# Batch 0 of a fused attention and MLP kernel: one head pair per load on two queues, an order that keeps one port apart, and w_in issued behind q

## The chip, the cores and the metric

The kernel runs on one core of one Trainium2 chip. The metric is the device time of one execution in microseconds (us), as a median over several executions. The core has five engines that run side by side, each through its own queue in order: TensorE (PE in the profile, its weight loads PEld), VectorE (DVE), ScalarE (ACT), GpSimd (POOL) and SyncE (SP, here only DMA issues). DMAs are issued from SP's, ACT's and POOL's queues; those of POOL can change the type on the way (float32 to bf16).

## The reference

```
scale = 1 / sqrt(sqrt(64))                  # q, k, v: 8 batches x 8 heads x 576 x 64
phi(x) = exp(h - max(h)) / sqrt(128),  h = x @ omega.T - |x|^2 / 2
kv  = phi(k).T @ v;   z = sum(phi(k))
att = (phi(q) @ kv) / (phi(q) @ z + 1e-6)
x   = att, heads side by side               # 4608 x 512
h   = x @ w_in                              # 512 x 2048
out = (h * clip(h + 3, 0, 6) / 6) @ w_out   # 2048 x 512, float32 out
```

The row factor of phi(q) drops out of num / den, so q's maximum isn't computed. k's row factor is kept as one reciprocal per row of k, and is multiplied into v.

## The kernel before

One list of operations is written down for all eight batches (`_emit`), each with its engines, an estimated duration, a priority, what it reads and what it writes. `Prog.schedule` (L104) then goes through it with a model of the chip and fixes, before anything runs, on which engine each operation is and in which order each engine takes its own. What is fixed is the order alone: at run time an operation starts when its engine has come to it and the semaphores that it waits for are there. Matmuls on a tile of ones (`idle_work`, L463, "fills") are put on PE by the planner where it thinks PE would have nothing to do; they keep PE's clock up, and take their time even where the planner was wrong.

A batch is 576 rows of 8 heads: four pairs of heads (m = 0 to 3, `NP`), for each pair 512 rows of each head in the "mains" and 64 in the "left-overs" (`l`). For batch 0, names as used in this document (the digit after the first point is the batch, the one after that the pair):

- `load` (L491) issues the DMAs of k, q, v as float32; batch 0 has the list `FIRST` (L337): k's mains, k's left-overs, q's mains, v's left-overs, v's mains, q's left-overs. Each mains DMA is one head of two pairs (`HALVES`), 256 KB. The first four DMAs go alternately to SP and ACT, the rest to SP.
- `cast` (L573) makes bf16 of k and q (castk, castq), `turns` (L576) transposes on PE (Tk, Tq) and copies back from PSUM (Tevk, Tevq).
- K0.u (L639, two matmuls each, nine groups of four chunks) projects k; eK0.u (L645, ACT) is the exponential; mx0.u (L648, DVE) the maximum; cc.0.m (L746) and ccl (L675) are reciprocals.
- vc.0.m (L750) multiplies v by the reciprocals, 128x512; vcl (L679, two instructions) does that for the left-overs; vcc (L754) writes the reciprocals beside them.
- Q0 (L656, PE) and eQ0 (L660, ACT) do q's side.
- kv.0.m (L763, L765) needs vc.0.m, vcc.0.m and vcl; kvz.0.m (L417 or L418) copies it from PSUM; num.0.mA and B (L791) multiply with phi(q), A and B being the first and second half of the rows; rec and div (L803, L807, DVE) divide; X.0.mA and B (L429) transpose the result and Xev copies it to xT.
- mm1 (batch 0: `mm1_half`, L884, in halves 0A and 0B of the rows; later L859) and mm2 (L917) are the two matmuls of the MLP. A batch's MLP runs beside the attention of the next.

`w_in_piece` (L474) and `w_out_piece` (L481) issue the weights from POOL's queue, four pieces of 512 KB each (wi0 to wi3, wo0 to wo3). wi0 and wi1 wait for v's left-overs of batch 0, wi2 and wi3 for v's last mains (`W_GATE`, L339). Batch 1's k, q, v wait for wi1, wi2, wi3, and w_out waits for batch 1's k. From batch 1 on k and q are cast by POOL's DMAs; from batch 2 on the transposes are DMAs too.

The lists of engines that an operation may go to are `EV0` (L16) for batch 0 and `EV_V` and others (L344 to L350) after it: vc and vcl may go to POOL or DVE. The planner takes, of the operations that an engine could start next, the one of the best priority among those that could start within `URGENT` (0.8 us) of the earliest, and puts another in front if that ends at most `FIT` (0.05 us) after it could start (L198 to L202).

Of the kernel before, what the change touches and what calls it, by code (L numbers as in the profile page):

```python
# [5 lines left out]
BF16 = mybir.dt.bfloat16  # L6
# [5 lines left out]

URGENT = 0.8
FIT = 0.05
IDLE_UNTIL = 21.0
# [27 lines left out]
class Prog:  # L43
# [60 lines left out]
    def schedule(self):  # L104
# [9 lines left out]
        queues = {}  # L114
        clock = [0.0]

        def flow(until, keep):
# [55 lines left out]
        while len(order) < n:  # L173
            best = None
            for e, lst in engines.items():
                cand = []
                for o in lst:
                    s = slot_of(o) if o.alloc else (0.0, ())
                    if s is None:
                        continue  # L180
                    cand.append((max(free[e], ready(o), s[0]), o, s[1]))
                if not cand:
                    continue
                idle = [x for x in cand if x[1].name == "idle"]
                cand = [x for x in cand if x[1].name != "idle"]
                m = min([x[0] for x in cand] + [1e9])
                if idle and (not cand or idle[0][0] + (0.02 if idle[0][0] < 8.0 else idle[0][1].occ) <= m):
                    if idle[0][0] > IDLE_UNTIL:
                        if not cand:
                            continue  # L190
                    elif best is None or idle[0][0] < best[0]:
                        best = (idle[0][0], e, idle[0][1], idle[0][2])
                        continue
                    else:
                        continue
                if not cand:
                    continue
                c = min((x for x in cand if x[0] <= m + (URGENT if x[1].prio < -1.0 else 0.02)),  # L198
                        key=lambda x: (x[1].prio, x[1].seq))
                fits = [x for x in cand if x[0] + (x[1].occ[e] if isinstance(x[1].occ, dict) else x[1].occ) <= c[0] + FIT]  # L200
                if c[0] > m + 0.02 and fits:
                    c = min(fits, key=lambda x: (x[1].prio, x[1].seq))  # L202
                if best is None or c[0] < best[0]:
                    best = (c[0], e, c[1], c[2])
            if best is None and all(o.name == "idle" for l in engines.values() for o in l):
                break
            if best is None:
                raise RuntimeError("stuck: " + str([(e, [o.name for o in l][:5]) for e, l in engines.items()]))
            st, e, o, picks = best
            for x in o.engs:  # L210
                engines[x].remove(o)
            o.eng = e
            occ = o.occ[e] if isinstance(o.occ, dict) else o.occ
            for vx, i in zip(o.alloc, picks):
                old = vx.ring.held[i]
                if old is not None:
                    for d in old.users:
                        o.deps.setdefault(d, False)
                vx.slot = i
                vx.ring.held[i] = vx  # L220
            o.start = st
            if o.group is not None:
                free[e] = st + o.issue
                flow(free[e], True)
                queues.setdefault(e, []).append([o, occ, free[e] + (1.25 if e == "POOL" else 0.9)])
                flow(1e9, False)
            else:
                free[e] = st + occ
                o.end = free[e]
            for vx in o.virts:  # L230
                vx.left -= 1
                vx.free_at = max(vx.free_at, o.end + o.lat)
            order.append(o)
            for s in o.succ:
                s.ndep -= 1
                if s.ndep == 0:
                    add(s)
# [81 lines left out]
def _emit(nc, es, q, k, v, omega, w_in, w_out, out):  # L319
# [13 lines left out]
    TU = [(0, 2), (2, 6), (6, 10), (10, 14), (14, 18)]  # L333
    HALVES = [(0, 2), (2, 4)]
    SPLIT = 3
    LATE = 0.4
    FIRST = [("k", 1), ("k", 0), ("q", 1), ("v", 0), ("v", 1), ("q", 0)]  # L337
    REST = [("k", 1), ("k", 0), ("q", 1), ("q", 0), ("v", 0), ("v", 1)]
    W_GATE = [("vl", 0)]*2+[("v32", 1, 3)]*2  # L339
    alpha = float(D) ** -0.25  # L340
    PE_T, PE_X = 2, 2
    SPARE = 1
    IDLE = (16, 60)
    EV_T = ("DVE", "ACT")  # L344
# [25 lines left out]
    kp = [sbt("kp%d" % u, [128, NCH, M], BF16) for u in range(2)]  # L370
    mx = [sbt("mx%d" % u, [128, NCH], F32) for u in range(2)]
    cc = [sbt("cc%d" % u, [128, NCH], F32) for u in range(2)]
    vc = [sbt("vc%d" % u, [128, 520], BF16) for u in range(2)]
# [100 lines left out]
    def w_in_piece(i, gate):  # L474
        f0, f1 = WI[i]
        op("POOL", 0.72 * (f1 - f0), lambda E: E.dma_start(
            wi[:, :, 128 * f0:128 * f1], w_in[:, 128 * f0:128 * f1].rearrange("(c p) f -> p c f", p=128)),
           -8.6 + 0.05 * i, reads=gate, writes=[("wi", i)], group="dwi%d" % i, inc=16, lat=1.0, name="wi%d" % i,
           issue=0.85, packet=91.0)

    def w_out_piece(g, gate):  # L481
        op("POOL", 2.95, lambda E: E.dma_start(
            wo[:, 4 * g:4 * g + 4, :], w_out[512 * g:512 * g + 512, :].rearrange("(c p) e -> p c e", p=128)),
           -0.2 + 0.05 * g, reads=gate, writes=[("wo", g)], group="dwo%d" % g, inc=16, lat=1.0, name="wo%d" % g,
           issue=0.85, packet=91.0)
# [5 lines left out]
    def load(b, eng, gates):  # L491
        pb = b % 2
        halves = HALVES if b == 0 else [(0, NP)]
        turn_of = [0]

        def dma(part, dst, src, n, keys, gate, prio, run):
            cast = b > 0 and part[0] in "kq"
            e = "POOL" if cast else eng[turn_of[0]] if turn_of[0] < len(eng) else "SP"
            op(e, n * (0.74 if b == 0 else 0.8) * (1.0 if run == 1024 else 1.5) / 262144.0,
               lambda E: E.dma_start(dst, src), prio + 0.001 * turn_of[0], reads=gate + (free if cast else []), writes=keys,  # L500
# [15 lines left out]
        def mains(t, src, dst):  # L516
            for x, (m0, m1) in enumerate(halves):
                for hh in range(2):
                    first = 64 * hh if t != "q" else 0
                    d = dst[:].rearrange("p m (h r) d -> p m h (r d)", h=2) if t == "v" else mains_of(dst)  # L520
                    rows = src[b, 2 * m0 + hh:2 * m1 - 1 + hh:2, first:first + MAIN, :]
                    dma("%s%d%d" % (t, hh, x), d[:, m0:m1, hh, :], rows.rearrange("m (p r) d -> p m (r d)", r=4),
                        131072 * (m1 - m0), landing(t, hh, m0, m1), gates[t], base[t], 1024)

# [20 lines left out]
    def attention(b):  # L545
# [19 lines left out]

        def four(m0, m1, hh):
            return [2 + 4 * m + 2 * hh + s for m in range(m0, m1) for s in range(2)]

        def every(m0, m1, s):
# [20 lines left out]

        def dbls(t):
            return t[:, 2:, :].rearrange("p (m h s) t -> p m h (s t)", h=2, s=2)

        def alts(t, s, m0, m1):
# [8 lines left out]
        if b == 0:  # L603
            for m0, m1 in HALVES:
                for hh in range(2):
                    nm = "%d%d" % (m0 // 2, hh)
                    dbl = four(m0, m1, hh)
                    cast("k", nm, 512, mains_of(kb)[:, m0:m1, hh, :], mains_of(k32)[:, m0:m1, hh, :],
                         main_keys("k", range(m0, m1), [hh]), dbl, 0)
                    turns("k", nm, dbl, dbls(kT)[:, m0:m1, hh, :], kb, 0)  # L610
            for s in range(2):
# [22 lines left out]
        for u in range(NU):  # L634
            vK = Virt(ring)

            def e_K(E, u=u, vK=vK):
# [9 lines left out]
               pos(u) + 0.02, reads=[vK], writes=[("kp", pb, u)], name="eK%d.%d" % (b, u))  # L647
            op("DVE", dvet(512), lambda E, u=u: E.reduce_max(  # L648
                mx[pb][:, 4 * u:4 * u + 4], kp[pb][:, 4 * u:4 * u + 4, :], axis=AX.X),
               pos(u) + 0.03, reads=[("kp", pb, u)], writes=[("mx", pb, u)], name="mx%d.%d" % (b, u))  # L650

# [25 lines left out]
        for hh in range(2):  # L677
            p0 = 64 * hh
            op(EV_V if b else V0, {"POOL": 0.62, "DVE": dvet(260)}, lambda E, hh=hh, p0=p0: E.tensor_tensor(  # L679
                vcl[pb][p0:p0 + 64, :, 65 * hh:65 * hh + 65], vl[pb][p0:p0 + 64, :, :],  # L680
# [57 lines left out]
    def pair(b, m, t):  # L738
# [10 lines left out]
        vcm = vc[u2][:].rearrange("p (c e) -> p c e", e=65)  # L749
        op(EV_V if b else V0, {"POOL": 1.2, "DVE": dvet(512)}, lambda E: E.tensor_tensor(  # L750
            vcm[:, :, 0:D], v32[:, m, :, :], cbc, ALU.mult),
# [187 lines left out]
    for b in range(B):  # L939
        if b == 0:  # L940
            load(0, ("SP", "ACT", "SP", "ACT"), {t: [] for t in "kqv"})
            for i in range(len(WI)):
# [72 lines left out]
```

The softmax here doesn't subtract the row's maximum and nothing guards it: scores larger than these inputs give would overflow.

## Time and profile before

| | |
|---|---|
| median of 6 runs | 323.96 us (323.75 to 325.13) |
| the profiled execution | 324.21 us, of which the span of instructions is 322.4 us |
| granted clock of PE over the span | 1.00 |
| busy: PE, DVE, ACT, POOL | 317.2, 209.1, 189.1, 77.0 us |

The profile shows one execution. A group of instructions is shown by line of the kernel, engine, operation and tile; "xcount" is how many, "mean ns" the length of one. Matmuls overlap, so that their own lengths are longer than the distance from one to the next: a 128x256 matmul is shown with 273 ns, and 14 of them take 1.73 us. Windows are stretches of the span, in us from its start. In a timeline a line stands for instructions of one kind in a row: its start, how long they take together, and in brackets how long the engine stood idle before them and what it waited for.

### The profile page before, as it was taken

How to read it: one execution, taken by the hardware profiler on the slowest of the kernel's cores; microseconds unless marked ns; L12 is line 12 of the kernel's file. 1: busy time of each engine (PE TensorE's matmuls, PEld its weight loads, DVE VectorE, ACT ScalarE, POOL GpSimd, SP SyncE). 2: the span in 40 equal slices, each digit the busy share in tenths (PEclk: the TensorE clock that was granted, in tenths of full speed). 3: DMA queues.
4: the chain of work that ended last, by engine and by line, in shares of the span. 5: the costliest groups of instructions: out<-in, count | busy, mean ns of one | idle time of the engine just before them, and what ended most of it. 6: DMA issues, size and time to landing. Idle time of an engine off the chain costs nothing.

```text
span 322.4 us, 5873 instructions
## 1 busy us (share of the span) xinstructions
PE 317.2 (98%) x2236; PEld 174.8 (54%) x2236; DVE 209.1 (65%) x460; ACT 189.1 (59%) x385; POOL 77.0 (24%) x107
## 2 busy tenths in 40 slices
PE   8999999999999999999999999999999999999996
PEld 6788855455654544565555545555555444444443
DVE  4988995597787947995796468846866353433411
ACT  3997892596595616966775387647674354344400
POOL 2775171065041600730334022402020000000000
PEclk9999999999999999999999999999999999999999
DMA  7999989999950999898929972998012201000024
GB/s 246 265 204 212 235 130 233 230 166 193 217 129 36 123 201 256 94 189 126 238 24 173 200 219 33 184 199 232 16 50 66 74 23 45 33 35 33 33 67 98
DMA packets 91532, 44.79 MB, mean 139 GB/s; under 512 B 58096, under 2 KB 87024, under 8 KB 91504
## 3 DMA queue, kind: packets, MB, share of 16 engines
q1 hardware_dynamic: 64288, 31.31, 42.4%
q0 software_dynamic: 26512, 12.46, 31.2%
q10 hardware_dynamic: 704, 0.66, 0.6%
q8 instruction: 18, 0.29, 0.4%
q14 instruction: 10, 0.08, 0.1%
HBM read 36.73 MB, written 9.44 MB: 143 GB/s over the span
## 4 chain that ended last, share of the span: by engine, by line
PE 92%; DVE 2%; DMA 2%; SPq 2%; POOL 1%; issue 0%; ACT 0%; POOLq 0%
PE p L917 39%; PE p L859 34%; PE p L656 5%; PE p L884 4%; PE p L639 4%; PE p L791 3%; PE p L763 2%; DMA v<-in_v_dram 2%; SPq L500 2%; DVE mx L648 1%; PE p L429 1%; PE p L765 1%; DVE vc L750 0%; POOL vc L750 0%; DVE vcl L679 0%
## 5 line engine op out<-in xcount | busy, mean ns | idle before, releaser
L917 PE MATMUL p<-wo,gT 128*128 128x512 bf16 (+2 forms) x592 | 141.0, 374 | 0.3 <-DVE qT L418 0.3
L867 DVE SCALAR_TENSOR_TENSOR gT<-tsb,p 128x512 bf16<-128x512 bf16 x128 | 86.8, 685 | 56.7 <-ACT tsb L865 55.9
L865 ACT ACTIVATE tsb<-p 128x512 bf16<-128x512 f32 x128 | 76.3, 602 | 71.1 <-PE p L859 71.0
L859 PE MATMUL p<-xT,wi 128*128 128x512 bf16 x448 | 107.3, 379 | 0.0
L917 PEld LDWEIGHTS p<-wo,gT 128*128 128x128 bf16 x592 | 56.2, 98 | 57.5 <-DVE qT L418 0.5
L859 PEld LDWEIGHTS p<-xT,wi 128*128 128x128 bf16 x448 | 42.6, 98 | 45.4
L648 DVE TENSOR_REDUCE mx<-kp 128x4 f32<-128x512 bf16 x72 | 46.7, 673 | 9.7 <-ACT kp L645 9.4
L645 ACT ACTIVATE kp<-p 128x512 bf16<-128x512 f32 x72 | 40.0, 621 | 15.2 <-PE p L639 15.1
L660 ACT ACTIVATE qpT<-p 128x512 bf16<-128x512 f32 (+1 forms) x80 | 41.6, 576 | 5.2 <-PE p L656 5.0
L750 POOL TENSOR_TENSOR vc<-v,cc 128x512 bf16<-128x512 f32 x22 | 23.5, 1067 | 36.9 <-DVE cc L746 27.4
L807 DVE TENSOR_TENSOR xb<-p,rec 128x384 bf16<-128x384 f32 (+1 forms) x64 | 28.5, 477 | 0.0
L639 PE MATMUL p<-om,kT 128*128 128x256 bf16 x144 | 23.0, 273 | 0.0
L656 PE MATMUL p<-qT,om 128*128 128x512 bf16 (+1 forms) x80 | 22.8, 358 | 0.0
L418 DVE COPY osb<-p 128x512 f32<-128x512 f32 (+2 forms) x12 | 7.8, 647 | 22.7 <-PE p L917 22.7
L417 ACT COPY osb<-p 128x512 f32<-128x512 f32 x25 | 14.8, 591 | 11.3 <-PE p L917 11.3
L639 PEld LDWEIGHTS p<-om,kT 128*128 128x128 bf16 x144 | 13.8, 98 | 9.7
L500 POOL DMA_DIRECT2D k<-in_k_dram x12 | 9.1, 770 | 41.6 <-PE p L859 33.7
L791 PEld LDWEIGHTS p<-kvz,qpT 128*128 128x128 bf16 x312 | 13.5, 98 | 5.8 <-ACT qpT L660 0.2
L859 PE MATMUL p<-xS,wi 128*128 128x512 bf16 x64 | 16.4, 379 | 0.0
L884 PE MATMUL p<-xT,wi 128*128 128x256 bf16 x128 | 15.9, 273 | 0.0
L763 PEld LDWEIGHTS p<-vc,kp 128*128 128x128 bf16 x256 | 11.9, 98 | 6.6 <-POOL vcl L679 0.7
L791 PE MATMUL p<-kvz,qpT 128*128 128x65 bf16 x312 | 14.8, 194 | 0.0
(69 smaller groups left out, 216.6 us busy)
## 6 DMA issues: line engine op xcount, KB each, us to landing
out_dram<-osb SPq DMA_DIRECT2D x32, 256.0 KB, 2.7
v<-in_v_dram SPq DMA_DIRECT2D x14, 512.0 KB, 5.3
wi<-in_moe_w_in_dram POOLq DMA_DIRECT2D x4, 512.0 KB, 8.1
k<-in_k_dram POOLq DMA_DIRECT2D x8, 256.0 KB, 5.3
k<-in_q_dram POOLq DMA_DIRECT2D x8, 256.0 KB, 6.5
wo<-in_moe_w_out_dram POOLq DMA_DIRECT2D x4, 512.0 KB, 13.3
kb<-in_k_dram POOLq DMA_DIRECT2D x6, 256.0 KB, 5.7
qb<-in_q_dram POOLq DMA_DIRECT2D x6, 256.0 KB, 7.8
```

Of the source, the lines that this page charges most:

```text
L639: ins = E.matmul(ring.t[vK.slot][:, 256 * i:256 * i + 256], kT[:, 2 * u + i, :], om[:].rearrange("d t m -> d (t m)"), start=True, stop=True)
L645: op("ACT", actt(512), lambda E, u=u, vK=vK: E.activation(kp[pb][:, 4 * u:4 * u + 4, :].rearrange("p c m -> p (c m)"), ring.t[vK.slot], AF ...
L648: op("DVE", dvet(512), lambda E, u=u: E.reduce_max(mx[pb][:, 4 * u:4 * u + 4], kp[pb][:, 4 * u:4 * u + 4, :], axis=AX.X), pos(u) + 0.03, r ...
L656: op("PE", mmt(n), lambda E, vQ=vQ, lh=lh: E.matmul(ring.t[vQ.slot][:, 0:n], om[:, lh, :], src, start=True, stop=True), p + 0.045 * lh, re ...
L660: op("ACT", actt(n), lambda E, vQ=vQ, lh=lh: E.activation(dst(lh), ring.t[vQ.slot][:, 0:n].rearrange("m (j t) -> m j t", t=128), AF.Exp, s ...
L791: ins = E.matmul(d[:, hh, i - i0, :], qpT[pb][:, o:o + 128], kvz[m][:, 65 * hh:65 * hh + 65], start=True, stop=True)
L807: op("DVE", dvet(128 * n), lambda E: E.tensor_tensor(xv(i0, i1), psum()[:, :, :, 0:64], rbc, ALU.mult), t + 0.01, reads=[vn, ("rec", ru)], ...
L859: ins = E.matmul(ring.t[vh.slot], wi[:, c, 128 * f:128 * f + 128], xv[:, c, :], start=(c == 0), stop=(c == NJ - 1))
L865: op("ACT", actt(512), lambda E: E.activation(tsb[tu][:], ring.t[vh.slot], AF.Relu, bias=0.5, scale=1.0 / 6.0), t - 0.1, reads=[vh], write ...
L867: op("DVE", dvet(512), lambda E: E.scalar_tensor_tensor(gT[gu][:, f, :], tsb[tu][:], 1.0, ring.t[vh.slot], ALU.min, ALU.mult), t - 0.1, re ...
L884: ins = E.matmul(ring.t[vh.slot][:, 256 * g:256 * g + 256], wi[:, c, 128 * (f + g):128 * (f + g) + 128], xT[0][:, c, 256 * half:256 * half ...
L917: ins = E.matmul(ring.t[vo.slot][:, 0:c1 - c0], gT[gu][:, f, 128 * tc:128 * tc + 128], wo[:, f, c0:c1], start=(f == 0), stop=(f == NF - 1))
```

## The change

- Batch 0's loads: k's pairs 0 and 1 come one head of one pair per DMA (128 KB), pairs 2 and 3 both heads of one pair per DMA (256 KB); q's as before, one head of two pairs; v's both heads of one pair. The first eight DMAs alternate between SP and ACT (four on ACT: k's head 1 of pairs 0 and 1, k's pair 3, q's first), the rest is on SP. k's casts and transposes in batch 0 follow these pieces (`KPARTS`).
- All four pieces of w_in wait for q's last mains.
- The planner: a POOL operation is not started before DVE's last operation named vc, vcl, cast or fold has ended, and such a DVE operation not before POOL's last. PE's operations are counted twice as long between 4 and 6 us. `URGENT` goes to 0.5, `FIT` to 0.1, and some estimated durations change (vc on POOL 1.2 to 1.32, vcl 0.62 to 0.72, the weights' DMAs).
- A folded form of the maximum is written down for batches below `FOLD`; `FOLD` is 0, so there is none.

Because the planner decides, each engine's order changes from the start to the end of the kernel. What the builds of both kernels hold for batch 0:

| | before | after |
|---|---|---|
| fills on PE | 63 | 65 |
| fills ahead of the first Tk | 18 | 14 |
| vc.0 on POOL, on DVE | 1, 3 | 4, 0 |
| vcl.0 on POOL | 2 | 2 |
| POOL, from its second castq | castq0.0B, wi0, wi1, vcl x2, wi2, wi3, castq0.1B, vc.0.2, castq0.l | castq0.0B, wi0 to wi3, vc.0.0, vcl x2, vc.0.1, vc.0.2, vc.0.3 |
| ACT, to the first Tevq | castk x2, eK0 x9, castq0.1A, Tevq0.0A | castk0.11 (256 columns), castk0.20 (512), eK0.1 to 0.3, Tevk0.l, eK0 x6, castq0.1A, vcc x2, castq0.1B, Tevq0.1A |
| eQ0 on ACT ahead of its first kvz | 2 (kvz.0.0) | 8 (kvz.0.3) |
| first mm2 of batch 0 on PE | each group of four matmuls of two row blocks in turn, with Q, kv, num between | the four groups of the first row block within one stretch |

Later batches: before, POOL has 21 of 28 vc and 7 of 14 vcl; after, all of both.

```diff
-URGENT = 0.8
-FIT = 0.05
+COLD = 6.0
+URGENT = 0.5
+FIT = 0.1
...
+        port = {"POOL": 0.0, "DVE": 0.0}
+
+        def shares(o, e):
+            return e == "POOL" or e == "DVE" and o.name.startswith(("vc", "cast", "fold")) and not o.name.startswith("vcc")
+
+        def held(o, e):
+            return port["DVE" if e == "POOL" else "POOL"] if shares(o, e) else 0.0
...
-                    cand.append((max(free[e], ready(o), s[0]), o, s[1]))
+                    cand.append((max(free[e], ready(o), s[0], held(o, e)), o, s[1]))
...
+            if e == "PE" and 4.0 < st < COLD:
+                occ *= 2.0
...
+            if shares(o, e):
+                port[e] = free[e]
...
+    PARTS = {"k": [(0, 1, 0, 1), (0, 1, 1, 2)] + [(1, 2, 0, 1), (1, 2, 1, 2)] + [(m, m + 1, 0, 2) for m in range(2, NP)],
+             "q": [(0, 2, 0, 1), (0, 2, 1, 2), (2, 4, 0, 1), (2, 4, 1, 2)],
+             "v": [(m, m + 1, 0, 2) for m in range(NP)]}
+    KPARTS = [(m, h0, h1) for m, _, h0, h1 in PARTS["k"]]
...
-    W_GATE = [("vl", 0)]*2+[("v32", 1, 3)]*2
+    W_GATE = [("q32", 1, 3)] * 4
...
-        op("POOL", 0.72 * (f1 - f0), lambda E: E.dma_start(
+        op("POOL", 0.64 * (f1 - f0), lambda E: E.dma_start(
...
-            for x, (m0, m1) in enumerate(halves):
-                for hh in range(2):
+            for m0, m1, h0, h1 in PARTS[t] if b == 0 else [(0, NP, 0, 1), (0, NP, 1, 2)]:
...
-            for m0, m1 in HALVES:
-                for hh in range(2):
-                    nm = "%d%d" % (m0 // 2, hh)
-                    dbl = four(m0, m1, hh)
...
+            for m, h0, h1 in KPARTS:
+                nm = "%d%d" % (m, h0)
+                dbl = [2 + 4 * m + x for x in range(2 * h0, 2 * h1)]
...
-        op(EV_V if b else V0, {"POOL": 1.2, "DVE": dvet(512)}, lambda E: E.tensor_tensor(
+        op(EV_V if b else V0, {"POOL": 1.32, "DVE": dvet(512)}, lambda E: E.tensor_tensor(
...
-            load(0, ("SP", "ACT", "SP", "ACT"), {t: [] for t in "kqv"})
+            load(0, ("SP", "ACT") * 4, {t: [] for t in "kqv"})
```

## The prediction

> **What bounds the kernel now.** I read the page's busy times first, then the windows, then PE's waits.
>
> ```profile
> PE 317.2 (98%) x2236; PEld 174.8 (54%) x2236; DVE 209.1 (65%) x460; ACT 189.1 (59%) x385; POOL 77.0 (24%) x107
> ```
> ```profile
> 24.00:40.00 16.00, 15.89 (x172) 14.32 (x170) 13.92 (x28) 12.78 (x26) 5.30 (x9) 1.00 1.34 223
> 40.00:60.00 20.00, 19.71 (x172) 10.90 (x171) 12.60 (x36) 11.09 (x27) 8.23 (x11) 1.00 1.15 195
> 60.00:100.00 40.00, 40.00 (x286) 21.74 (x285) 30.41 (x71) 29.71 (x65) 14.07 (x17) 1.00 0.95 166
> ```
> ```profile
> PE p L466 <- DVE fill L461: 1.3, 1, 1.3
> PE p L763 <- POOL vcl L679: 0.4, 1, 0.4
> PE p L917 <- DVE qT L418: 0.3, 1, 0.3
> ```
>
> The second figure of a window is PE's busy time. From 24 us on PE lacks 0.11 + 0.29 = 0.40 us, and then nothing until 300. PE's matmuls are the same in both kernels, so there the change can win 0.4 us at most; what it gives beside that is decided by how early PE has its real work without gaps. PE counts as busy in the first 24 us only because of 63 fills. The page cannot show what that hides, so I look at the engines one by one: POOL from 11 to 19 us, two DVE rows, ACT's exponentials.
>
> ```profile
> 10.98 1.69 POOL L476 DMA_DIRECT2D wi<-in_moe_w_in_dram  x2 [1.07 <-DMA vl<-in_v_dram]
> 12.68 1.74 POOL L679 TENSOR_TENSOR vcl<-vl,cc 64x260 bf16<-64x260 f32 x2
> 14.37 1.55 POOL L476 DMA_DIRECT2D wi<-in_moe_w_in_dram  x2
> 15.96 0.61 POOL L418 CAST qb<-q 128x512 bf16<-128x512 f32 x1
> 16.66 1.46 POOL L750 TENSOR_TENSOR vc<-v,cc 128x512 bf16<-128x512 f32 x1
> ```
> ```profile
> 12.28 0.98 DVE L750 TENSOR_TENSOR vc<-v,cc 128x512 bf16<-128x512 f32 x1 [0.19 <-DVE cc L746]
> 14.36 0.68 DVE L750 TENSOR_TENSOR vc<-v,cc 128x512 bf16<-128x512 f32 x1
> 9.12 3.54 ACT L645 ACTIVATE kp<-p 128x512 bf16<-128x512 f32 x7 [0.39 <-PE p L639]
> ```
>
> Beside POOL's vcl, DVE's vc takes 0.98 us instead of 0.68; beside DVE's vc, POOL's takes 1.46, and the median over all 22 on POOL is 1.04. Castq on POOL beside DVE's maxima (8.62 to 9.91) took 0.645 each against 0.61 alone. So it is vc and vcl that disturb each other, and the planner's new rule names the right pair. ACT in a row does an exponential every 0.51 us.
>
> **k's pieces: ACT, price 0.** ACT issues four DMAs of 0.5 us instead of two, so its table load (1.28) ends at 4.0 instead of 3.0; nothing had landed for it before 3.6. Its second operation is castk0.20, ahead of every exponential. k20 is third on SP behind omega and two 128 KB pieces: 544 KB, as much as up to the last k DMA before.
>
> ```profile
> k<-in_k_dram SPq DMA_DIRECT2D x1, 256.0 KB, 4.9
> q<-in_q_dram SPq DMA_DIRECT2D x1, 256.0 KB, 5.9
> ```
>
> That one was issued at 1.66 and landed at 6.6. Now ACT's queue carries 768 KB beside it instead of 512, so it may come as late as k's left-overs did (2.17 + 4.9 = 7.1); it comes earlier only if two queues move more than one. I take 6.8: cast to 7.45, first exponential at 7.5, against 7.54 before. The early small pieces thus win nothing on ACT. Nine exponentials (4.6) and Tevk0.l, which moves to ACT (0.37), end at 12.5; castq0.1A, two vcc and castq0.1B (0.62, 0.35, 0.6) follow, Tevq0.1A ends at 14.6.
>
> By the Trainium skill, DMA: Bandwidth & Descriptors, Anatomy of one DMA, a DMA costs about 2.0 us before its bytes; the two DMAs more that k has would, laid one behind the other, make 4 us and 328 us in all. The trace has the queue of 256 KB pieces moving 340 GB/s from 4 to 5 us and 369 from 6 to 7, many under way at once, so I price the two at their issues alone (0.5 each, beside transfers).
>
> **w_in: POOL.** q's last mains were issued at 4.26 and landed 5.9 later, at 10.16; v's left-overs landed at 10.69 and POOL went on 0.29 later. So wi0 is issued at 10.45 instead of 10.98, and all four issues (1.69 + 1.55) stand ahead of vc.0.0: until 13.7. v's first mains (11.4 before) are there by then. vc.0.0 at 1.04 and two vcl at 0.62 end at 16.1, and kv.0.0 can start, against 14.48 before. Three more vc at 1.04 and the gaps end at 19.35; the last vc was done at 18.12 before. The removed disturbance (0.30 + 0.42 + 0.43) is less than what goes from DVE to POOL in series.
>
> By the Trainium skill, GPSIMD Engine Reference, Engine selection, an elementwise operation of two inputs belongs on VectorE, being about twice as slow on GpSimd. The rows say 1.04 against 0.69, 1.5 times. By the page the four vc would end 1.3 us later, and kv.0.3 with them, some 0.8 of it uncovered, and I would say 325.3; the sum goes by the rows.
>
> w_in's own landing moves little: wi0 landed 6.4 after its issue (17.4), the others 2.5 apart. Even unmoved it leads the first mm1 (20.0 in both). Bounds: 0.5 earlier to 0.5 later, both covered. If that cover were gone, the first mm1 would wait that long.
>
> **PE.** From the distances between starts (0.108 for 256 columns, 0.216 for 512, 0.057 for a transpose, 0.32 for a kv, 0.15 for half a num) I count what PE must do. Before, from the first K0 (7.1) to X.0.3B: 40 fills, 4.3, and 11.1 of work: 22.5 without a wait. The trace has X.0.3B at 23.65; waits were 1.15, most hidden in the overlap. After: PE reaches Tk0.30 at 7.25, then has 50 fills, 5.4, and 10.0 of work up to X.0.3B: 22.65 without a wait. Behind X.0.3B it has four mm1 matmuls more than before and one Q0 less: 0.33. So the start comes at 22.65 + 0.33 - 23.65 = -0.67 plus the new waits:
>
> - K0.0 waits for Tevk0.l on ACT, K0.5 and Tk0.l for the k pieces: 0.55.
> - Q0.1A waits for Tevq0.1A, 14.6; with the wait for castq0.1B ahead of it: 0.5. Twelve fills follow, and PE comes to kv.0.0 at about 16.7. POOL was ready at 16.1 and is covered by 0.6.
> - From kv.0.0 on, kvz, num, rec, div and X of a pair go round PE and DVE (0.27, 0.18, 0.41, 0.29 and about 0.2 for each hand-over) and four X or mm1 parts come 0.1 to 0.25 early: 0.55.
>
> Together 1.6, X.0.3B at 24.25, the full stream 0.9 later. Unknown are these waits; below, 0.3 if k20 lands half a us earlier and the planner is right elsewhere, above, 2.6 if it lands one later. I take 1.6, nearer to before's 1.15 than to 2.6.
>
> **From 24 us on.** Batch 1's transposes come three mm1 groups sooner in PE's order, and mm1 groups are left to put between Tq1; that covers the 0.40: minus 0.4 (bounds 0 and -0.4). But mm2's four first groups now stand within 5 us. w_out landed at 38.6, 41.1, 43.8 and 46.3; counted on, PE comes to them at 41.1, 42.2, 44.2 and 46.0. So 0.3 may be lost on the last; w_out's chain of loads starts with w_in, somewhat earlier, so I take 0 of 0 to 0.3. All vc of later batches on POOL cost DVE nothing and POOL 7 x 1.04 and 7 x 0.62 more in some 200 us, beside PE's work: 0; without that cover each late vc holds PE, which is in order.
>
> **Sum.** 0.9 - 0.4 = +0.5 on the profiled execution's 324.21: 324.7. That execution stands 0.25 over the median of the runs, so the median becomes 324.5. About 0.2% (0.65 us) is what can be told from no change here; this forecast lies just inside.
>
> **Rivals.**
> - *The planner is right, PE waits hardly at all.* Waits of 0.3 make -0.37, with the 0.4 behind: 323.2. For it: the counts, in which the order without waits beats before, fewer fills at the slow start, and POOL undisturbed. Against: before, the planner was off by 1.15 too. It decides if k20 lands before about 6.2.
> - *k20 comes late, ACT holds everything.* One mechanism: castk0.20 ahead of all exponentials. Each us past 6.8 goes through exponentials, castq, Tevq0.1A and kv to the end, since nothing on that path is slack. At 7.8: 325.5. It is slower than 0.2% from 7.0 on, given the other terms. For it: ACT's queue now carries half as much again beside SP's. Against: window 6 to 7 moved 369 GB/s, the queues are not at their slowest there.
> - *It gives back what it takes.* DMA engines are busy throughout from 3 to 40 us (mean share over 1), w_out's landing sets when mm2 can run whatever the start was, and both kernels meet there: 324.0.
>
> **How the numbers follow.** Forecast 0.46 (324.05 to 324.95: half of it inside 0.2%, half slower); planner right 0.26 (faster, with a little inside); k20 late 0.20 (slower); given back 0.08 (mostly inside). Faster 0.27, same 0.30, slower 0.43. Range: 322.8 (no wait, 0.4 won, a little of the port) to 325.9 (waits 2.6 and the 0.3 at w_out). The forecast alone: 324.05 to 324.95.
>
> **What would show it.** Right: the first exponential at 7.3 to 7.7; wi0 to wi3 issued in one row from 10.4; POOL's vc at 1.04 and vcl at 0.62; kv.0.0 at 16.5 to 17; X.0.3B at 24 to 24.5; no PE wait beyond 0.1 from 24 to 60. Wrong: X.0.3B before 23.4 (planner right), exponentials from 8 on (k20 late), PE waiting for wo or a vc behind a DMA issue after 40 us, or a wait in any window from 60 on, which I count nowhere.

## The result, and the profile after

| | before | after |
|---|---|---|
| median of the runs | 323.94 us (323.28 to 325.74, 67 runs) | 325.74 us (324.69 to 326.96, 30 runs) |
| ratio to before | | 1.0049, 95% interval 1.0040 to 1.0058 |
| the profiled execution | 324.21 us, span 322.4 | 326.96 us, span 325.2 |

The change makes the kernel 0.49% slower, 1.8 us in the medians. The execution that was profiled is the longest of after's 30 and stands 1.2 us over their median, so the 2.8 us between the two spans is about one us more than the typical loss. The parts of the loss are read from it, their typical size from the runs further down.

The busy times, the three windows, and PE's waits of the changed kernel, in the views that the prediction began with (L447 is the transposes, L484 the fills, L936 mm2, as L429, L466 and L917 were):

```profile
PE 318.2 (98%) x2238; PEld 175.6 (54%) x2238; DVE 203.8 (63%) x456; ACT 185.8 (57%) x378; POOL 89.9 (28%) x122
```
```profile
24.00:40.00 16.00, 16.00 (x176) 14.58 (x174) 14.23 (x32) 12.85 (x27) 6.92 (x11) 1.00 1.31 214
40.00:60.00 20.00, 19.13 (x177) 11.22 (x175) 13.88 (x38) 9.23 (x22) 9.40 (x12) 1.00 1.30 201
60.00:100.00 40.00, 40.00 (x302) 22.13 (x301) 30.07 (x70) 29.28 (x65) 16.34 (x21) 1.00 0.93 173
```
```profile
PE p L447 <- POOL kb L436: 1.6, 1, 1.6
PE p L484 <- DVE fill L479: 1.3, 1, 1.3
PE p L936 <- DMA wo<-in_moe_w_out_dram: 0.9, 2, 0.5
```

DVE lost 5 us of work and POOL took 13, as the order says; neither sets the time. Before's two small waits behind 24 us are gone, and a new one of 0.9 us for w_out stands between 40 and 60 us: there PE is busy 19.13 of 20, where it was 19.71. Ahead of 7 us PE stands 1.6 us for a cast of k on POOL. The engines one by one, ACT's first operations and POOL's row from q's casts on:

```profile
8.34 0.62 ACT L435 CAST kb<-k 128x512 bf16<-128x512 f32 x1 [3.93 <-DMA k<-in_k_dram]
8.87 1.56 ACT L655 ACTIVATE kp<-p 128x512 bf16<-128x512 f32 x3
```
```profile
11.96 3.18 POOL L494 DMA_DIRECT2D wi<-in_moe_w_in_dram  x4 [0.47 <-DMA q<-in_q_dram]
15.12 1.09 POOL L769 TENSOR_TENSOR vc<-v,cc 128x512 bf16<-128x512 f32 x1
16.29 1.31 POOL L698 TENSOR_TENSOR vcl<-vl,cc 64x260 bf16<-64x260 f32 x2
17.68 1.04 POOL L769 TENSOR_TENSOR vc<-v,cc 128x512 bf16<-128x512 f32 x1
```

castk0.20 (the first row; in brackets, ACT stood 3.93 us for the DMA) starts at 8.34 and the first exponential at 8.87, where 7.5 was forecast. w_in goes out at 11.96 instead of 10.45. POOL's work itself is as forecast: 1.04 to 1.09 a vc, 1.31 for two vcl. kv.0.0 comes at 18.30 and X.0.3B at 25.38, 1.7 later than before.

Why k comes late is in the windows by single us (last column: GB/s that the DMA engines moved, the one ahead of it their mean busy share), first of before, then of after:

```profile
3.00:4.00 1.00, 1.00 (x7) 0.75 (x6) 0.19 (x2) 0.42 (x2) 0.00 (x0) 1.00 1.05 313
4.00:5.00 1.00, 1.00 (x7) 0.54 (x6) 0.58 (x2) 0.24 (x1) 0.11 (x1) 1.00 1.12 340
```
```profile
3.00:4.00 1.00, 1.00 (x7) 0.75 (x6) 0.23 (x2) 0.96 (x1) 0.54 (x2) 1.00 0.93 239
4.00:5.00 1.00, 1.00 (x9) 0.82 (x8) 0.73 (x3) 0.41 (x1) 0.25 (x1) 1.00 0.71 228
```

With the 128 KB pieces the DMA engines move a quarter to a third less between 3 and 5 us, and between 4 and 5 their share falls to 0.71: they have less to do than they could, while everything behind waits in the queues.

### The profile page after: what moved, and what is told of

It is laid out like the page before. It is cut to its first block, busy times and chain, and to the rows that moved or that the text cites. A ratio compares the mean times of both kernels' runs of the same rounds, so it can differ in the third digit from the quotient of the medians.

```text
span 325.2 us, 5857 instructions
## 1 busy us (share of the span) xinstructions
PE 318.2 (98%) x2238; PEld 175.6 (54%) x2238; DVE 203.8 (63%) x456; ACT 185.8 (57%) x378; POOL 89.9 (28%) x122
## 4 chain that ended last, share of the span: by engine, by line
PE 82%; DMA 13%; POOL 2%; SPq 1%; issue 1%; DVE 0%; POOLq 0%
PE p L936 37%; PE p L878 33%; DMA wo<-in_moe_w_out_dram 5%; PE p L675 4%; PE p L649 3%; PE p L810 3%; DMA wi<-in_moe_w_in_dram 3%; DMA k<-in_k_dram 2%; DMA q<-in_q_dram 2%; PE p L782 2%; DMA v<-in_v_dram 1%; SPq L517 1%; POOL wo L500 1%; PE p L784 0%; POOL vc L769 0%
## 5 line engine op out<-in xcount | busy, mean ns | idle before, releaser
L936 PE MATMUL p<-wo,gT 128*128 128x512 bf16 (+2 forms) x592 | 142.0, 374 | 0.9 <-DMA wo<-in_moe_w_out_dram 0.9
L878 PE MATMUL p<-xT,wi 128*128 128x512 bf16 x448 | 109.8, 379 | 0.0
L936 PEld LDWEIGHTS p<-wo,gT 128*128 128x128 bf16 x592 | 56.0, 98 | 56.4 <-DMA wo<-in_moe_w_out_dram 1.8
L659 DVE TENSOR_REDUCE mx<-kp 128x4 f32<-128x512 bf16 x72 | 47.5, 679 | 20.3 <-ACT kp L655 20.3
L655 ACT ACTIVATE kp<-p 128x512 bf16<-128x512 f32 x72 | 41.6, 613 | 13.1 <-PE p L649 13.1
L769 POOL TENSOR_TENSOR vc<-v,cc 128x512 bf16<-128x512 f32 x32 | 33.6, 1051 | 34.3 <-DVE cc L765 20.1
L698 POOL TENSOR_TENSOR vcl<-vl,cc 64x260 bf16<-64x260 f32 x16 | 9.9, 616 | 63.6 <-DVE cc L694 32.0
L649 PE MATMUL p<-om,kT 128*128 128x256 bf16 x144 | 25.9, 281 | 0.0
L675 PE MATMUL p<-qT,om 128*128 128x512 bf16 (+1 forms) x80 | 23.7, 358 | 0.0
L436 DVE COPY osb<-p 128x512 f32<-128x512 f32 (+2 forms) x15 | 9.8, 656 | 21.7 <-PE p L936 21.5
L435 ACT COPY osb<-p 128x512 f32<-128x512 f32 x22 | 12.9, 586 | 6.0 <-PE p L936 6.0
```

Source lines behind the costliest of these rows:

```text
L649: ins = E.matmul(ring.t[vK.slot][:, 256 * i:256 * i + 256], kT[:, 2 * u + i, :], om[:].rearrange("d t m -> d (t m)"), start=True, stop=True)
L655: op("ACT", actt(512), lambda E, u=u, vK=vK: E.activation(kp[pb][:, 4 * u:4 * u + 4, :].rearrange("p c m -> p (c m)"), ring.t[vK.slot], AF ...
L659: op("DVE", dvet(512), lambda E, u=u: E.reduce_max(mx[pb][:, 4 * u:4 * u + 4], kp[pb][:, 4 * u:4 * u + 4, :], axis=AX.X), pos(u) + 0.03, r ...
L675: op("PE", mmt(n), lambda E, vQ=vQ, lh=lh: E.matmul(ring.t[vQ.slot][:, 0:n], om[:, lh, :], src, start=True, stop=True), p + 0.045 * lh, re ...
L769: op(EV_V if b else V0, {"POOL": 1.32, "DVE": dvet(512)}, lambda E: E.tensor_tensor(vcm[:, :, 0:D], v32[:, m, :, :], cbc, ALU.mult), t, re ...
L878: ins = E.matmul(ring.t[vh.slot], wi[:, c, 128 * f:128 * f + 128], xv[:, c, :], start=(c == 0), stop=(c == NJ - 1))
```

## The experiments

All ratios are to the kernel before on the same chip, which had 323.8 to 324.0 us there. "Pinned" means that the planner's order stays that of the kernel named, and only the DMAs are moved.

The first four runs ask why k and q come late: because two queues work at once (theory A), or because the pieces are small (theory B). The others ask what is left of the loss once the pieces are 256 KB again: w_out's estimate (theory W) or the new prologue (rival R); the last ones, what the parts are worth each by itself. A prologue is here what comes ahead of PE's first mm2.

| | median us (lowest to highest, runs) | ratio, 95% interval | X.0.3B us | wait for w_out us |
|---|---|---|---|---|
| after | 325.74 (324.69 to 326.96, 30) | 1.0049, 1.0040 to 1.0058 | 25.38 | 0.9 |
| e1 | 325.67 (325.44 to 326.07, 5) | 1.0058, 1.0043 to 1.0073 | 24.20 | 0.9 |
| e2 | 325.13 (324.30 to 326.62, 11) | 1.0037, 1.0022 to 1.0052 | 23.36 | 0.8 |
| e3 | 325.22 (324.81 to 326.56, 6) | 1.0047, 1.0028 to 1.0065 | 26.01 | 0 |
| e4 | 326.41 (325.68 to 328.41, 6) | 1.0087, 1.0064 to 1.0110 | 24.89 | 1.0 |
| e5 | 324.29 (323.69 to 324.99, 12) | 1.0005, 0.9992 to 1.0017 | 23.50 | 0 |
| e6 | 324.31 (323.58 to 325.58, 12) | 1.0001, 0.9985 to 1.0018 | 23.27 | 0 |
| e7 | 324.04 (323.74 to 327.49, 12) | 1.0004, 0.9983 to 1.0025 | 24.03 | 0 |
| e8 | 323.07 (322.87 to 325.66, 12) | 0.9980, 0.9959 to 1.0002 | 25.38 | 0 |
| e9 | 324.75 (323.82 to 326.39, 9) | 1.0031, 1.0011 to 1.0050 | 24.18 | 0 |
| e10 | 323.30 (322.95 to 323.77, 11) | 0.9984, 0.9973 to 0.9995 | 22.70 | 0 |
| e11 | 323.33 (322.94 to 323.59, 11) | 0.9979, 0.9969 to 0.9990 | 23.23 | 0 |
| e12 | 324.92 (324.32 to 325.58, 12) | 1.0030, 1.0017 to 1.0043 | 24.07 | 0 |

(X.0.3B and the wait are from one profiled execution each; before had 23.67 and no wait for w_out. One of e7's 12 runs took 677.91 us and isn't in the span given.)

**e1, fewer loads on ACT.** After, pinned; k's pair 3 and q's first go from ACT's queue to SP's:

```
    G.schedule()
+   for o in G.order:
+       if o.name in ("k30.0", "q00.0"): o.eng = "SP"
```

> The changed kernel with every engine's order as it is, but k's pair 3 and q's first load issued on SP: ACT keeps two loads of 128 KB, as many loads as before the change. In the changed kernel both hardware queues hold work until 7.5 us and the DMA engines are busy 0.70 to 0.85 from 3.5 to 5.5 us; q's last mains land at 11.65 instead of 10.16. Theory A (two queues with work on both move less than one queue does): ACT runs dry by 4 us, SP alone moves some 180 KB per half us from then on, q's last lands by 10.6 and the time falls by 0.8 to 1.5 us, to 324.3 to 325. Theory B (the 128 KB pieces are slow, whatever the queue): q's last lands at 11.2 or later, the time stays within 0.4 us of 325.7. Theory C (the loads don't matter, the order does): q may land early and the time still stays at 325.7.

1.0058, not better than after. The first exponential comes at 8.06, and from 3.5 to 5.5 us the DMA engines move 154 GB/s, less than after's 221. How much lies on ACT's queue isn't the cause.

**e2, the same bytes in larger pieces.** After, pinned; the two heads of a pair in one DMA for pairs 0 and 1, as pairs 2 and 3 have it. The casts stay as they are, and ACT still carries 768 KB:

```
+   for m, keep, drop in ((0, "k00.0", "k01.0"), (1, "k11.0", "k10.0")):
+       # keep loads both heads of pair m (256 KB); drop is gone, who waited for it waits for keep
```

> The changed kernel with every engine's order as it is, but k's pairs 0 and 1 loaded by one DMA of 256 KB each (SP and ACT) instead of two of 128 KB; ACT still carries 768 KB. Theory A (two queues): no better, q's last at 11.2 or later, time 325.4 to 326.2. Theory B (small pieces): q's last by 10.5, time 324.3 to 325. The first transposes start later in either case (first piece by about 3.9 instead of 3.0), which PE's fills cover.

1.0037. The windows of e2 and its two rows on ACT:

```profile
3.00:4.00 1.00, 1.00 (x7) 0.74 (x6) 0.30 (x2) 0.62 (x2) 0.00 (x0) 1.00 1.05 369
4.00:5.00 1.00, 0.60 (x4) 0.12 (x2) 0.58 (x2) 0.35 (x1) 0.22 (x1) 1.00 1.01 354
```
```profile
6.96 0.62 ACT L435 CAST kb<-k 128x512 bf16<-128x512 f32 x1 [2.61 <-DMA k<-in_k_dram]
7.49 1.56 ACT L655 ACTIVATE kp<-p 128x512 bf16<-128x512 f32 x3
```

369 and 354 GB/s instead of 239 and 228, on the same two queues (ACT's alone holds as many bytes as in after); the first exponential at 7.49, w_in at 10.41: what the prediction had. So the DMA engines starve because the same bytes come in small pieces, as theory B says. Smaller pieces are also more DMAs and more issues, and no run tells the size from the number. The time is less clear than the rate: 325.13 lies between the two theories' forecasts, and the intervals of e2 and of after overlap. Part of the reason is that a wait of 0.84 us for w_out stays, though w_out was issued at 28.04 here, as early as before (27.99).

**e3, two queues without small pieces.** Before, pinned; q's first two mains (256 KB each) go from SP's queue to ACT's, so that ACT has four:

```
    G.schedule()
+   for o in G.order:
+       if o.name in ("q00.0", "q01.0"): o.eng = "ACT"
```

> The kernel before with every engine's order as it is, but two of q's loads of 256 KB moved from SP to ACT, so that ACT carries 1024 KB in four loads as the changed kernel's ACT carries 768 KB in four. Theory A (two queues): q's last mains land at 11.2 or later instead of 10.16, v's behind them later by as much, and the time grows by 0.7 to 1.7 us, to 324.7 to 325.7. Theory B (small pieces): q's last within 0.4 us of 10.16, time within 0.4 of 323.95. ACT's table load is 1 us later in both, beside 0.6 us of idle time before its first cast, so up to 0.4 us on its first cast.

1.0047, the time that theory A forecast and B did not. It isn't A's mechanism, though: from 3.5 to 5.5 us the DMA engines move 350 GB/s, and q's last main lands at about 10.7, between the two forecasts. What comes late are k's left-overs, in rows of 256 bytes on SP's queue: between 5.5 and 6.5 us SP's queue moves 256 packets and 83 KB, ACT's 231 packets and some 220 KB, and PE stands 2.0 us for the left-overs' cast.

```profile
PE p L429 <- DVE kb L418: 2.0, 1, 2.0
```

(The profiled execution is the longest of the six; in it the clock also fell behind that standstill, see e8.) Two queues cost something here too, by another way than in after: they move about as many packets each, and the one with the short rows loses. The Trainium skill, DMA: Bandwidth & Descriptors, Queues, rings and completion order, says that SP and ACT have rings on the same 16 engines and that an engine goes round its queues packet by packet; the 256 packets beside 231 agree with that.

**e4, one queue for all.** After, pinned; all of batch 0's loads on SP:

```
+       if o.name in ("k01.0", "k11.0", "k30.0", "q00.0"): o.eng = "SP"
```

> The changed kernel with every engine's order as it is, but all of batch 0's loads on SP, ACT issues none. Theory A (two queues): one queue from the start moves 160 to 180 KB per half us as soon as its issues are ahead (0.47 us each, so the six k mains are issued by 4.0 us); q's last at 10 to 10.8, time 324.3 to 325.2. Theory B (small pieces): DMA engines starve from 3 to 5 us in spite of one queue, q's last at 11.2 or later, time 325.4 or more.

1.0087, worse than after. From 3.5 to 5.5 us one queue of small pieces moves 249 GB/s, more than after's two (221), and the first exponential comes at 7.57, as the prediction had it. What is late is q: with every issue on SP, q's last main goes out at 6.22 instead of 4.18 and lands at 11.79, w_in goes out at 12.09, and kv.0.0 waits 0.3 us for POOL's vcl. So a second queue is worth issue time here, not rate; and the loss has another path than in after, through w_in and POOL instead of the exponentials. Both of theory B's forecasts (q's last at 11.2 or later, 325.4 or more) came. At 0.47 us an issue, one queue can offer 128 KB pieces at no more than about 270 KB per us (an estimate), so the issues could explain e4's rate; they don't explain after's, where two queues issue.

**e5, w_out's estimate.** e2 with one number put back:

```
-        op("POOL", 2.56, lambda E: E.dma_start(
+        op("POOL", 2.95, lambda E: E.dma_start(
             wo[:, 4 * g:4 * g + 4, :], ...
```

> The version with both pairs' heads in one 256 KB DMA for k (e2: 325.13, PE waits 0.8 for w_out), and the planner's estimate of a w_out piece put back from 2.56 to 2.95 us. The prologue is the same operation for operation up to PE's first mm2; then the planner puts a group of mm2 of the second row block between the first two and the last two groups of the first row block, so that PE comes to w_out's third and fourth piece later. Theory W (what is left of the loss after the pieces of k is PE standing at w_out's landing, because the order trusts 2.56): the 0.8 us of waits between 40 and 60 us goes, 324.3. Rival R (w_out's landing sets mm2 in any order, and the loss lies in the new prologue: series of POOL, fills): a wait for w_out of 0.5 or more stays at the other group, 325.1.

1.0005: the wait is gone, and 0.8 us with it. PE's first mm2 in e2, and the window that the wait is in, of e2 and of e5:

```profile
43.20 1.04 PE L936 MATMUL p<-wo,gT 128*128 128x512 bf16 x4
...
46.04 0.81 PE L936 MATMUL p<-wo,gT 128*128 128x512 bf16 x3 [0.84 <-DMA wo<-in_moe_w_out_dram]
```
```profile
40.00:60.00 20.00, 19.02 (x165) 10.57 (x168) 12.21 (x34) 7.81 (x18) 7.45 (x11) 1.00 1.26 219
```
```profile
40.00:60.00 20.00, 20.00 (x175) 11.03 (x173) 12.99 (x35) 8.54 (x19) 7.90 (x11) 1.00 1.31 232
```

Theory W holds here. With 2.95 the planner puts a group of the second row block in between, and PE comes to the group of w_out's fourth piece at 46.92. In e2 the four groups of the first row block stand in one stretch: PE was there at 45.20, 0.84 ahead of the piece. The prediction had counted 46.0 and a landing at 46.3; the piece came as counted, PE sooner, since e2's X.0.3B is 0.9 earlier than the 24.25 of the sum.

**e6, the gate alone; e7, the rules alone; e8, both.** On the kernel before, with its loads and its estimates of the weights' DMAs.

```
e6, e8:
-    W_GATE = [("vl", 0)]*2+[("v32", 1, 3)]*2
+    W_GATE = [("q32", 1, 3)] * 4
e7, e8: URGENT, FIT, COLD, port/shares/held, the estimates of vc and vcl on POOL, as in the change
```

> The kernel before with the gate of w_in alone changed (all four pieces behind q's last mains); loads, rules and estimates as before. The planner answers with vcl once on POOL and once on DVE, vc.0.1 and vc.0.3 on POOL. Theory W: the gate costs nothing by itself, w_in moves data only once the loads have drained; start and w_out as before, 323.9 (within 0.4). Rival R (four issues in a row ahead of POOL's vc and vcl are what holds kv): X.0.3B 1 us later, 324.9.

> The kernel before with the planner's rules and the estimates of vc and vcl on POOL changed (URGENT, FIT, the rule for one port, PE counted twice to 6 us); loads, gate and the estimates of the weights' DMAs as before. All vc and vcl of batch 0 go to POOL in one row behind wi3; 28 fills between Q0 and kv instead of 11. Theory W: the order costs little, since POOL undisturbed gives back what the row takes: 324.1 (323.7 to 324.5). Rival R (POOL's row is longer than what it replaces and sets kv.0.3): X.0.3B 0.8 us later than the 23.65 of before, 324.8 with no wait for w_out.

> The kernel before with both the gate and the planner's rules, loads and the estimates of the weights' DMAs as before: the change without its pieces of k and without its optimistic w_out. Theory W: 324.0 (323.6 to 324.5), X.0.3B within 0.5 of 23.65 and no wait for w_out above 0.3. Rival R: 325, as the version with 256 KB pieces of k (325.13) which differs in loads and w_out's estimate alone.

1.0001, 1.0004 and 0.9980. Neither the gate nor the rules cost anything: on before's loads rival R is out three times. (The rules also hold a condition that the diff at the start leaves out: between 4.8 and 8 us the planner puts a fill only where it sees 0.2 us or more without work, where before it put one from 0.02. It belongs to what e7 and e8 test, and bears on the standstill below.) In e7 the vc of batch 0 in one row on POOL come late by the profile (X.0.3B at 24.03), and PE's stream behind 24 us without any wait gives it back. Of e8's 12 runs nine took 322.87 to 323.73 and three 325.08 to 325.66 (the expectation of e11 says eight and four); the profiled one was of the three. So most were faster than theory W's forecast, and the profiled X.0.3B of 25.38 missed it. The windows of that execution and the wait that leads there (the column ahead of the last two is PE's granted clock):

```profile
7.81 0.59 PE L441 MATMUL p<-ident,kb 128*128 128x128 bf16 x6 [1.53 <-POOL kb L430]
```
```profile
5.00:8.00 3.00, 1.42 (x16) 0.77 (x13) 0.79 (x2) 1.22 (x4) 0.61 (x1) 1.00 1.09 327
8.00:12.00 4.00, 4.00 (x29) 2.97 (x27) 3.56 (x8) 3.30 (x8) 2.23 (x4) 0.57 1.13 329
12.00:16.00 4.00, 4.00 (x42) 3.46 (x40) 3.56 (x11) 3.12 (x9) 3.86 (x5) 1.00 1.16 195
```

PE stands 1.53 us for castk0.10 (k landed late in this run), and then runs at half its clock for some 3.4 us. Half of 3.4 us of 322 is 0.5%, so the mean granted clock over the span falls to 0.995. That mark stands in two of the three long runs and in none of the nine; the third (325.08) has 1.00.

**e9, w_out's estimate in the whole change.** After with 2.95 instead of 2.56, the edit of e5.

> The changed kernel with nothing undone but the planner's estimate of a w_out piece (2.95 again instead of 2.56): the loads of k in 128 KB pieces stay, the prologue is the changed kernel's own up to the first mm2. Theory W (two separate prices, 128 KB pieces and w_out's estimate, that add up): its ratio to the kernel before is the changed kernel's 1.0049 less the 0.0032 that the same edit took from the version with 256 KB pieces (1.0037 to 1.0005): 1.0017, 324.5, no wait for w_out above 0.3. Rival R (in the changed kernel w_out lands 1 us later than with 256 KB pieces, so that even the later order meets it): a wait of 0.5 or more stays, 325.2.

1.0031: the wait is gone and 0.6 us of the 1.6 that the ratio stands for. Theory W had 1.0017 and R 1.004; the point lies between, and the interval holds the first. Three of the nine runs (325.63, 325.75 and 326.39) bear the mark of a fall of the clock, 0.995 over the span; the other six, picked afterwards, have 1.0019 in the mean, near W's forecast. What is left is the first 24 us: the first exponential is at 8.31, X.0.3B at 24.18. Against e5, which differs in the pieces of pairs 0 and 1 alone, the small pieces cost 1.0031 - 1.0005, 0.26%; by the six runs it would be 0.14%, and after against e2 makes 0.12%. The intervals are about as wide as these differences.

**e10, all but the loads.** e8 with the change's estimates of w_out and w_in as well:

```
-        op("POOL", 0.72 * (f1 - f0), ...        # w_in
+        op("POOL", 0.64 * (f1 - f0), ...
-        op("POOL", 2.95, ...                    # w_out
+        op("POOL", 2.56, ...
```

> The whole change but its loads: gate, rules and all estimates (w_out 2.56, w_in 0.64) on the loads of before. The planner again puts groups of one row block close together. Theory W: the wait for w_out comes back, 0.8 to 1.0 between 40 and 60 us, and the time is that of the version with gate and rules (ratio 0.998) plus 0.003: 1.001, 324.2. Rival R (the estimate did harm only because the start was late): no wait for w_out above 0.3, 323.2.

0.9984, faster than before, and no wait for w_out. The first exponential is at 6.78, w_in goes out at 9.81, w_out at 27.51 (after: 30.56). But this doesn't decide between W and R, because the condition of the expectation did not come about: the planner did not put the four groups of one row block together. As in e5 and e9, a group of the second row block stands between the first two and the last two.

```profile
40.00:60.00 20.00, 20.00 (x172) 10.86 (x172) 12.12 (x32) 7.57 (x17) 7.16 (x9) 1.00 1.28 228
```
```profile
43.57 1.03 PE L929 MATMUL p<-wo,gT 128*128 128x512 bf16 x4
...
45.26 1.04 PE L929 MATMUL p<-wo,gT 128*128 128x512 bf16 x4
```

The fourth piece of w_out was issued at about 29.75 and took 15.5, so it landed at about 45.2. PE came to its group at 45.26. Had that group stood where the one before it does, at 43.57, PE would have waited for the piece (an estimate from these two times; no run has that order on these loads). What the run does show is that the estimate of 2.56 does no harm by itself: it harms through the order that it leads to.

So with the change's loads the ratio is 1.0049, and without them 0.9984. The 0.65% between is 2.1 us, but it holds two things: the loads, and the order of mm2 that the planner makes for them. The chain of runs e10 (0.9984), e5 (1.0005), e9 (1.0031), after (1.0049) parts it: 0.21% from before's loads to the change's with 256 KB pieces, 0.26% for the small pieces, 0.18% for w_out's order, each with a wide interval. One estimate of the change is left as before in e8 and e10 (0.8 for a piece of the later batches' loads, 0.74 in the change); no run moved it alone.

**e11, the standstill bridged.** e8 with six of the 24 fills behind Tq0.0B moved ahead of Tk0.10; as many matmuls as before:

```
+    for gone in [the first 6 of the 24 fills behind Tq0.0B]: G.order.remove(gone)
+    # the fill ahead of K0.2 goes behind it and issues 7 matmuls instead of 1
```

> The version with gate and rules on the loads of before, with six of the 24 fills behind Tq0.0B moved ahead of Tk0.10, where PE stood for 1.53 us in the profile of that version, the clock fell to 0.50 for 3.4 us behind it, and 4 of 12 runs took 325 to 325.7 where the other 8 took 322.9 to 323.7. Theory C (those slow runs are the clock's fall after the standstill): no granted clock below 1.00 behind 7 us, all runs within 322.8 to 323.8, median 323.0. Rival D (the slow runs come from elsewhere): runs above 325 stay, some 4 in 12.

0.9979, all 11 runs within 322.94 to 323.59, clock 1.00 throughout. That agrees with theory C, but doesn't show it: none of 11 beside three of 12 can be chance, e10 has no long run in 11 either though it has no bridge, and one of e8's three long runs has a clock of 1.00. The median is 0.47 us under the kernel before (323.80 beside it); e8, e10 and e11 can't be told apart by their intervals.

```profile
5.00:8.00 3.00, 2.67 (x30) 2.11 (x28) 1.06 (x4) 2.11 (x4) 0.61 (x1) 1.00 1.08 329
8.00:12.00 4.00, 3.90 (x41) 3.07 (x38) 4.00 (x12) 3.93 (x8) 2.88 (x4) 1.00 1.13 328
```

**e12, the loads alone.** Before with the change's loads and k's casts and transposes by these pieces; gate, rules and estimates of before:

```
+    PARTS = {...}; KPARTS = [...]
-            load(0, ("SP", "ACT", "SP", "ACT"), {t: [] for t in "kqv"})
+            load(0, ("SP", "ACT") * 4, {t: [] for t in "kqv"})
```

> The kernel before with the change's loads alone (pieces, casts and transposes of k by these pieces, eight DMAs alternating between SP and ACT); gate, rules and estimates of before, w_out's 2.95 among them. Theory L (the loads are the whole loss, and they delay q and so w_in and everything POOL sends after it): the ratio of the changed kernel with 2.95 (1.0031) less that of gate and rules (0.998), 1.005, 325.4; X.0.3B at 24.2 or later; w_out issued 1 us or more behind the 27.99 of before. Rival M (the pieces do harm only where all four of w_in stand behind q, and where ACT's castk0.20 stands ahead of every exponential; here castk0.20 is on POOL): 324.2, X.0.3B within 0.3 of 23.67.

1.0030, between the two: the loads cost 0.3% by themselves (w_out goes out 1.14 later than before, X.0.3B 0.4 later), not the 0.5% of theory L. Here ACT's first full cast is castk0.30, the exponentials start at 7.08, and w_out has 2.95. The parts don't add: 1.0030 with 0.9984 would make 1.0014, and the change is 1.0049. e9 puts about half of the 0.35% between at w_out's estimate. The other half fits the exponentials, which in the change's order stand behind a late castk0.20 (8.87 and 8.31 in after and e9), but no run moved castk0.20 alone; the falls of the clock in e9 are a rival for it.

## Why the prediction was right and wrong

The time lies within the range (322.8 to 325.9), 0.16 us under its upper end, and slower was the likeliest sign; the likeliest time, 324.5, was 1.24 us short. That it stayed in the range is partly luck: waits counted 0.9 too high hid part of what the late k20 and a wait priced at 0 cost. By the runs, about 0.6 to 0.8 of the 1.24 is the order around w_out and the rest the late loads. By its own steps:

- *k's pieces, price 0; k20 at 6.8.* **This step failed.** It took the queue of 256 KB pieces (340 and 369 GB/s) as the price of 128 KB pieces. From 3.5 to 5.5 us after's DMA engines move 221 GB/s and e2's 348. k20 landed at 8.3, and what came was the rival "k20 comes late, ACT holds everything", with its point of decision (7.0) passed. Its reason was wrong, though: not ACT's queue carrying more (e1 takes that away and gains nothing), but the small pieces (e2). By its rate of one us for one, a landing at 8.3 makes 326.0; the profiled execution, 326.96, less the 0.87 lost at w_out, is 326.1. This is one execution, the longest of the 30.
- *Each us goes through to the end.* Held where nothing else was late. From the first exponential to X.0.3B it is 15.9 us in e2, e5, e9, e10 and e11, with first exponentials from 6.78 to 8.31; 16.1 in e1 and 16.5 in after. In e4, where q and w_in were late instead, it is 17.3.
- *The new waits, 1.6.* Too many. In e2, where k20 and w_in came as forecast (7.49, 10.41), kv.0.0 starts at 16.28 and X.0.3B at 23.36 instead of 24.25, so that 0.7 of waits stand over the count of 22.65. This error hid part of the first.
- *w_out, 0 of 0 to 0.3.* **This step failed too:** 0.9 in after, 0.84 in e2. The step saw the four first groups of mm2 close together, and took w_out's chain as earlier. In after it was later: w_out was issued 2.57 us behind before's. In e2 it was issued as before, and PE came early instead. The median pays 0.6 to 0.8 for it (e9, e5); with a group of the second row block in between, the wait is gone on the same loads.
- *0.4 of old waits won.* Held: in e5, e7, e8, e10 and e11 PE is busy 16.00 of 16 and 20.00 of 20 from 24 to 60 us.
- *POOL's rows and w_in's four issues.* Held: 3.18 for four issues, 1.09, 1.31. The port rule does what it says, and gate and rules together are what gains (e8, e11). With vc at 1.04 to 1.09, the 325.3 said for a GpSimd twice as slow lies near the median by luck; and the 328 said for two DMAs laid one behind the other did not come.
- *The sum.* With the measured terms: X.0.3B 1.71 later, 0.33 of work behind it, 0.4 won, 0.87 lost at w_out make +2.5 on the span of 322.4; the span is 325.2. For e2 the same sum is 0.02 - 0.4 + 0.84, 322.9 against 322.8.

## What to carry to other kernels

Price a load that starts a kernel at the rate which pieces of its own size reach there, not at the rate of larger pieces in a full queue: halving some of the pieces here took the rate from about 350 to 221 GB/s, and moved what came after them. An estimate in a planner acts through the order that it leads to: the same 2.56 went with a wait in after and e2, and with none in e10, where the planner made another order. So look at the order that was built, before trusting what a changed estimate is said to do. Where fills keep PE busy, it may pay to put them into the stretch whose end is uncertain, since a standstill there can cost the clock as well; e11 agrees with that and doesn't prove it.

## What the runs showed of the hardware that was not expected

- **Small pieces.** From 3.5 to 5.5 us the five kernels that begin with 128 KB pieces of k moved 154 to 270 GB/s (after, e1, e4, e9, e12), the nine with 256 KB pieces alone 317 to 353. The Trainium skill, DMA: Bandwidth & Descriptors, Bandwidth, gives 138 GB/s for a DMA of 64 KB and 341 for one of 1 MB, both issued from GpSimd, and asks for 1 MB and more. The order of sizes agrees; but here 256 KB pieces from SP and ACT, several under way, moved 317 to 353.
- **The clock falls after a shorter standstill than thought.** 1.53 us without work brought PE to 0.50 from about 8.6 to 12.0 us (e8), 2.02 us from about 9.6 to 13.0 (e3). After's standstill of 1.58 left it at 1.00, so length alone doesn't decide; what does was not tried. Each is one execution. The Trainium skill, TensorE: Matmul & The Clock Gate, Why this matters for your kernels, warns of gaps above about 3 us; in these two executions 1.53 and 2.02 us were enough. Its free-running window of 3.4 us (What's actually happening) fits the 3.4 us that both falls lasted.
- **POOL's weights wait for the loads, whenever issued.** In after w_in is issued from 11.96, and POOL's queue moves 47 KB from 13.5 to 14.5 us, while SP's last loads run out, then 164 and from there about 200 KB per us; in e10, issued from 9.81, it moves 131 KB from 12.5 to 13.5. w_in, batch 1's k and q and w_out all follow one behind the other, so what the first loads lose can come out at w_out 30 us later: in after it goes out 2.57 us behind before's.
